# Convolution with channels on the partitions, turned into rows by VectorE

## The chip, the cores and the metric

The kernel runs on one core of a Trainium2 chip. The metric is the device time in microseconds of one execution, as a median of several. TensorE (PE in the profile) does the matmuls and PEld loads their weights; VectorE is DVE, ScalarE is ACT, GpSimd is POOL, and SyncE (SP) issues most transfers. Everything is float32.

## The reference

```python
# x: 8 x 3584 x 192; 8 heads of 24 channels, 7 taps
w = softmax(weight, axis=-1)                    # per head
x = out[b, s] = sum_k w[head, k] * x_pad[b, s + k]      # causal, per channel
# mixture of 8 experts, F = 1024
logits = x @ w_gate
local_gate = sigmoid(x @ w_local)
for b in range(B):
    prev_e = -1
    for s in range(S):
        fresh_e = argmax(logits[b, s])
        e = fresh_e if s == 0 or local_gate[b, s] < 0.5 else prev_e
        prev_e = e
        p = softmax(logits[b, s])
        h = np.maximum(x[b, s] @ w1[e], 0.0)
        out[b, s] = p[e] * (h @ w2[e])
```

A token takes the expert of its own logits or that of the token before it. So the choice is a scan along the sequence, and the tokens must be sorted by expert before the two matmuls with the expert's weights.

## The kernel before

The 28672 tokens are cut into 16 groups of 1792 (`PT`, 128 partitions x 14 tokens). Groups 0 and 1 are convolved by PE at the start (`wide`). Groups 2 to 15 go through these steps:

- `load_x` brings a group's x in one transfer on SP's queue: each partition has 14 tokens and the 6 before them, 192 channels each.
- `conv` makes the convolution with tokens on the partitions. For each of the 8 heads ACT writes the first tap (`first`, L413), and DVE adds the other six (L423, 128 x 336 elements, in place in `y_sb`).
- `logits` turns the rows by DVE transposes of 32 x 32 blocks (`z`, L606), so that channels lie on the partitions. 48 matmuls (L620) with 64 x 32 tiles follow: six slices of channels, four column groups, two halves of the rows. ACT copies the two results to `ls`, DVE turns them back (`lq`, L628), and sixteen small copies put them in order in `lt` (by DVE, L644, or by ACT, L642, where `aside` holds).
- `route` finds expert and factor of each token on DVE, and the slot at which its row is to lie. `put` scatters the 14 rows of `y_sb` a partition to the table `slots` in HBM (L828, POOL's queue). `tables` makes from the counts which block is of which expert.

The sorted rows are worked off in blocks. 28 blocks have one tile of 128 rows and 43 have two (`hidden` L1047, `output` L1068). The 23 large blocks after them have four tiles, and a few smaller ones end the run. Before a block its weights (1.5 MB) and its rows are loaded on SP's queue. `hidden` and `output` split the 128 rows of the contraction into two halves of 64 (`halves`), which run side by side.

A large block computes the hidden layer in `seven`: two by two parts of it, by sums and differences of parts of x and of the weights, in 11 products (`times`, L1211) instead of 12. The three PSUM pairs `xb`, `wbk` and `yb` collect them. ACT copies three intermediate results out (L1217, L1223 and L1225, the last from `xb` to `h12`). DVE then adds `wbk` to `h11` (L1230), `xb` to `h22` (L1233) and `yb` to `h12` (L1242), and ACT applies the ReLU. `output_late` (L1259) follows; its first part writes the PSUM pool that `yb` came from. The pieces `h11` to `h22` are parts of the old tile `hot`, and the sums lie in pieces of old `xg` and `hT` tiles, which is why the profile has these names.

The order of all this is set while the program is written out. `step(time)` is called at fixed places in each block. It takes operations of `route` or `conv` (generators that yield an estimate in microseconds for each DVE operation) until the time given is used up. A yielded "pe" or "hop" hands over to the other generator until the next place. `SIDE` holds the times of the large blocks' four places; the first lies ahead of the additions in `seven`. `start_conv` and `start_route` say when a group may begin:

```python
        free = not any(p[0] <= g - 3 for p in to_put)
        if (st["cgen"] is None and g < NPART and g <= st["route"] + LEAD and free ...
        ...
        if st["rgen"] is None and st["route"] < done:
```

The rows `y_sb` of a group lie in one of four (later three) buffers `ys`, and `z` in the one buffer `yt`.

Of the kernel before, what the change touches and what calls it, by code (L numbers as in the profile page):

```python
# [8 lines left out]
F32 = mybir.dt.float32  # L9
I32 = mybir.dt.int32  # L10
Act = mybir.ActivationFunctionType
# [6 lines left out]
P = 128  # L18
# [3 lines left out]
GS = D // H  # L22
# [73 lines left out]
TQ = (NT + 3) // 4  # L96
WA = F * KD // 2
# [14 lines left out]
def kernel(  # L112
# [4 lines left out]
    weight: bass.AP,  # L117
    wh: bass.AP,
# [49 lines left out]
    c = cst.tile([P, H, KC], F32, name="c")  # L168
    nm = cst.tile([P, H], F32, name="nm")
    rz = cst.tile([P, H], F32, name="rz")  # L170
    with tc.tile_pool(name="scr", bufs=1) as scr:
        w = scr.tile([1, H, KC], F32, name="w")
        nc.scalar.dma_start(out=w, in_=weight.rearrange("(o h) k -> o h k", o=1))

        nc.sync.dma_start(out=hank, in_=wh)
        x_in = {0: load_b(0)}
        wg = cst.tile([P, 3 + DQ, Q], F32, name="wg")
# [15 lines left out]
        wide_w = scr.tile([P, 2 * H + H * KC], F32, name="wide_w")  # L193
# [9 lines left out]
        wc = ws[:, H:].rearrange("o (h k) -> o h k", k=KC)  # L203
        nc.vector.tensor_tensor(w, w, bcast(wm, KC), op=Alu.add)
        nc.scalar.activation(w, w, Act.Exp)
# [5 lines left out]
        nc.vector.tensor_tensor(wc, w, bcast(ws[:, :H], KC), op=Alu.mult)  # L211
        cps = hps_p.tile([P, 512], F32, name="hps")
        nc.tensor.matmul(cps[:, :H + H * KC], lhsT=ones, rhs=wide_w[:, H:], start=True, stop=True)
# [3 lines left out]
    wgb, wgq = wg[:, :3, :], wg[:, 3:, :]  # L217
# [180 lines left out]
    def row_tile(g):  # L398
        at = g % 4 if g < NARROW else (g + 1) % 3
        return ys[at].tile([P, NB, DG], F32, name="y_sb")  # L400

    def conv(g, x_sb):
        y_sb = row_tile(g)[:, :NT, :]
        got[g] = y_sb

        def cols(h):
            return y_sb[:, :, Y0 + h * GS:Y0 + (h + 1) * GS]

        def chans(h, k):
            return x_sb[:, k:k + NT, h * GS:(h + 1) * GS]  # L410

        def first(h):
            nc.scalar.activation(cols(h), chans(h, 0), Act.Copy, scale=c[:, h, 0:1])  # L413

        first(0)
        yield 0
        for h in range(H):
            if h + 1 < H:
                first(h + 1)
            if h == H // 2 and 2 < g < NPART - 1:  # L420
                x_in[g + 1] = load_x(g + 1)
            for k in range(1, KC):
                nc.vector.scalar_tensor_tensor(cols(h), chans(h, k), c[:, h, k:k + 1],  # L423
                                               cols(h), Alu.mult, Alu.add)
                yield 0.6
# [175 lines left out]
    def logits(g, y_sb):  # L601

        z = z_tile()[:, :NT * D].rearrange("p (t d) -> p t d", d=D)
        for t in range(0, NT, TQ):
            u = min(t + TQ, NT)
            nc.vector.transpose(z[:, t:u, :], y_sb[:, t:u, Y0:Y0 + D])  # L606
            yield 0.2 * (u - t)
        yield "pe"


        if late_p:
            both = st["bank"].tile([P, 2, 512], F32, name="ps")
            lps = [both[:, half, :TQ * Q] for half in range(2)]
        else:
            lps = [hps_p.tile([P, TQ * Q], F32, name="hps") for half in range(2)]
        begin = [min(TQ * j, NT - TQ) for j in range(4)]
        for b in range(DQ):
            for j in range(4):
                for half, rows in halves():
# [978 lines left out]
```

## Time and profile before

| | |
|---|---|
| median of 3 runs | 1312.2 us (1310.24 to 1314.26) |
| profiled execution, its own time | 1310.09 us |
| its span | 1308.3 us |
| PE busy | 1274.2 us, 97% |
| DVE busy | 956.2 us, 73% |
| ACT busy | 618.7 us, 47% |
| POOL busy | 551.8 us, 42% |
| mean granted PE clock | 0.996 |

The span runs from the first to the last instruction of the profiled execution. Busy time counts overlapping instructions of an engine once. A row of costs gives line, engine, operation, what is written and read, the shape and the count, then busy microseconds in all, nanoseconds of one, and the idle time just before with what ended it. A matmul of float32 appears as two records.

### The profile page before, as it was taken

What the parts mean: (1) busy time and instruction counts of PE and PEld (TensorE: products, weight loads), DVE (VectorE), ACT (ScalarE), POOL (GpSimd) and SP (SyncE); (2) the same over time, 40 slices, a digit from 0 to 9 for tenths busy, and PEclk for the clock granted to TensorE, in tenths of its full rate; (3) what the DMA queues carried; (4) which work ended last, traced back from release to release, by engine and by line L of the source; (5) the groups of instructions that cost most, each with busy time, mean ns of one, the idle gap of its engine ahead of it and who ended that gap; (6) DMA issues with size and microseconds to landing.
All of it is one profiled execution on the core that took longest, in us unless ns stands there. A gap on an engine that the chain in (4) does not pass through costs nothing. (4 is left out here: it accounts for less than half of the span.)

```text
span 1308.3 us, 40023 instructions
## 1 busy us (share of the span) xinstructions
PE 1274.2 (97%) x15750; PEld 1215.0 (93%) x15750; DVE 956.2 (73%) x2602; ACT 618.7 (47%) x1384; POOL 551.8 (42%) x619
## 2 busy tenths in 40 slices
PE   9899999999999999999999999999999999999997
PEld 7799999999999999899999899999999899999996
DVE  6888898889888888788988898889857844431111
ACT  5345555445555645456464454454343434432332
POOL 4444443534344444444445633644462664421211
PEclk9999999999999999999999999999999999999999
DMA  5789998857767767667696655554555637536894
GB/s 198 279 338 382 375 345 345 295 201 270 259 217 260 264 211 266 221 223 261 206 280 178 171 165 152 152 147 149 127 170 119 192 110 183 157 92 195 269 314 164
DMA packets 130244, 291.18 MB, mean 223 GB/s; under 512 B 87936, under 2 KB 104759, under 8 KB 114306
## 3 DMA queue, kind: packets, MB, share of 16 engines
q1 hardware_dynamic: 107728, 243.35, 56.5%
q0 software_dynamic: 22320, 45.22, 10.3%
q8 instruction: 126, 2.06, 0.7%
q14 instruction: 68, 0.56, 0.1%
q10 hardware_dynamic: 2, 0.00, 0.0%
HBM read 242.92 MB, written 46.07 MB: 221 GB/s over the span
## 5 line engine op out<-in xcount | busy, mean ns | idle before, releaser
L423 DVE SCALAR_TENSOR_TENSOR y_sb<-x_sb,c,y_sb 128x336 f32<-128x336 f32 x672 | 383.1, 579 | 33.9 <-ACT y_sb L413 11.0
L1068 PE MATMUL yps<-wb,hT 64*128 64x192 f32 x3648 | 317.2, 325 | 5.9 <-ACT hT L1056 4.7
L828 POOL DMA_INDIRECT slots<-y_sb,posi x228 | 227.2, 996 | 210.4 <-PE yps L1068 148.4
L1047 PE MATMUL hps<-xT,wb 64*128 64x256 f32 (+1 forms) x3408 | 314.1, 336 | 1.7 <-issue 0.8
L1259 PE MATMUL ps<-wb,hot 64*128 64x192 f32 x3680 | 308.0, 323 | 0.1
L1068 PEld LDWEIGHTS yps<-wb,hT 64*128 64x128 f32 x3648 | 296.5, 187 | 10.4 <-ACT hT L1056 7.1
L1047 PEld LDWEIGHTS hps<-xT,wb 64*128 64x128 f32 x3408 | 279.4, 187 | 25.4 <-issue 4.3
L1259 PEld LDWEIGHTS ps<-wb,hot 64*128 64x128 f32 x3680 | 301.4, 187 | 1.5 <-issue 0.9
L1096 POOL DMA_INDIRECT out_dram<-o_sb,head x115 | 120.7, 1050 | 293.8 <-DVE o_sb L1274 268.1
L1056 ACT ACTIVATE hT<-hps 128x512 f32<-128x512 f32 (+1 forms) x284 | 130.7, 510 | 161.9 <-PE hps L1047 116.4
L1096 POOL DMA_INDIRECT out_dram<-o_sb,xg x114 | 117.2, 1028 | 209.5 <-DVE o_sb L1082 113.8
L1269 ACT ACTIVATE o_sb<-ps,head 128x192 f32<-128x192 f32 x115 | 42.9, 417 | 231.3 <-PE ps L1259 196.7
L1274 DVE SCALAR_TENSOR_TENSOR o_sb<-ps,head,o_sb 128x192 f32<-128x192 f32 x115 | 43.2, 412 | 104.6 <-ACT o_sb L1269 100.3
L1135 DVE STREAM_TRANSPOSE xT<-y_sb 128x768 f32<-128x768 f32 (+1 forms) x65 | 54.8, 870 | 77.3 <-DMA y_sb<-slots 31.4
L1029 ACT COPY xT<-xps 64x256 f32<-64x256 f32 (+4 forms) x284 | 105.1, 370 | 7.6 <-PE yps L1068 1.7
L1078 ACT ACTIVATE o_sb<-yps,xg 128x192 f32<-128x192 f32 x114 | 43.2, 418 | 125.1 <-PE yps L1068 82.9
L1211 PE MATMUL ps<-xT,wb 64*128 64x256 f32 x736 | 88.9, 377 | 0.8 <-DVE xT L1187 0.8
L1211 PEld LDWEIGHTS ps<-xT,wb 64*128 64x128 f32 x736 | 77.2, 187 | 2.6 <-issue 1.6
L1082 DVE SCALAR_TENSOR_TENSOR o_sb<-yps,xg,o_sb 128x192 f32<-128x192 f32 x114 | 43.4, 412 | 32.5 <-ACT o_sb L1078 27.2
L1156 PE MATMUL ps<-xT,wb 64*128 64x128 f32 (+1 forms) x912 | 64.5, 294 | 0.7 <-DVE xT L1135 0.6
L1156 PEld LDWEIGHTS ps<-xT,wb 64*128 64x128 f32 x912 | 62.6, 188 | 1.5 <-DVE xT L1135 1.5
L413 ACT ACTIVATE y_sb<-x_sb,c 128x336 f32<-128x336 f32 x112 | 63.1, 580 | 0.5
(281 smaller groups left out, 1301.2 us busy)
## 6 DMA issues: line engine op xcount, KB each, us to landing
wb<-in_w_dram SPq DMA_DIRECT2D x109, 1536.0 KB
x_sb<-in_x_dram SPq DMA_DIRECT2D x14, 1920.0 KB
y_sb<-slots SPq DMA_DIRECT2D x92, 192.0 KB
xg<-slots SPq DMA_DIRECT2D x43, 195.0 KB
wb<-in_w_dram SPq DMA_DIRECT2D x12, 512.0 KB
slots<-y_sb,posi POOLq DMA_INDIRECT x228
x_sb<-in_xb_dram SPq DMA_DIRECT2D x4, 768.0 KB
y_sb<-slots SPq DMA_DIRECT2D x60, 48.0 KB
```

The costliest lines, as they stand in the source:

```text
L413: nc.scalar.activation(cols(h), chans(h, 0), Act.Copy, scale=c[:, h, 0:1])
L423: nc.vector.scalar_tensor_tensor(cols(h), chans(h, k), c[:, h, k:k + 1], cols(h), Alu.mult, Alu.add)
L828: ins = nc.gpsimd.indirect_dma_start(out=slots[:, :], in_=rows, in_offset=None, out_offset=bass.IndirectOffsetOnAxis(ap=to, axis=0)).ins
L1029: copied = nc.scalar.copy(a, b)
L1047: ins = nc.tensor.matmul(hps[half][:, j, w], lhsT=wb[rows, f0:f0 + P], rhs=xT[rows, d, w], start=(d == 0 and j == 0), stop=(d == KD - 1), ...
L1056: nc.scalar.activation(hT[:, m:m + 2, w], hps[half][:, :, w], Act.Relu)
L1068: ins = nc.tensor.matmul(yps[half][:, k * D:(k + 1) * D], lhsT=hT[rows, m, k * P:(k + 1) * P], rhs=wb[rows, WA + m * D:WA + (m + 1) * D], ...
L1096: sent = nc.gpsimd.indirect_dma_start(out=out, in_=o, in_offset=None, out_offset=bass.IndirectOffsetOnAxis(ap=xg.bitcast(I32)[:, k, 1:2], ...
L1135: nc.vector.transpose(xT.rearrange("p d (j t) -> p j d t", t=Q)[:, js], rows[:, js].rearrange("p j (d t) -> p j d t", t=Q))
L1156: nc.tensor.matmul(hps[:, half, j, :], lhsT=wb[rows, f0:f0 + P], rhs=xT[rows, d, :], start=(d == 0 and j == 0), stop=(d == KD - 1), skip_g ...
L1211: ins = nc.tensor.matmul(to[:, half, j, :], lhsT=b[rows, j * P:(j + 1) * P], rhs=a[rows, :], start=(first and j == 0), stop=True, skip_gro ...
L1259: ins = nc.tensor.matmul(yps[:, half, k * D:(k + 1) * D], lhsT=h[two][rows, side, j, k * P:(k + 1) * P], rhs=wb[rows, f * D:(f + 1) * D], ...
```

## The change

Three things change.

First, the convolution. x comes in a layout made on the host: channel c of 32 on the partition, for each of the four quarters of the rows; then 6 slices of channels, and along each partition 20 x 32 tokens. A tap is then one scalar for each partition and slice (`c`, loaded as `taps` and normalized on the chip, `taps_done`). `conv` has 6 slices instead of 8 heads, with 448 contiguous elements each. Its result is already what the logits matmuls read (`z`; in `ys[2]` for even groups, in `yt` for odd ones). The rows `y_sb` are made from it afterwards, by DVE transposes of the same sizes as before.

Second, the logits. 12 matmuls over all 128 rows replace 48: six slices, two column groups of 64, 224 columns each. There is one copy to `ls`, one transpose, and eight small copies to `lt`.

Third, `seven`: the product a13 b31 is issued in two halves with s3 t3 between them, and `h22` is added ahead of `h11`. The ReLU of `h11` is made in two pieces and that of `h22` last.

With this the row buffers become three (later two), and the rules of starting change.

```diff
     def load_x(g):
-        x_sb = xs.tile([P, NX, D], F32, name="x_sb")
-        src = x[g // PER]
-        win = bass.AP(tensor=src.tensor, offset=src.offset + g % PER * PT * D,
-                      ap=[[NT * D, P], [1, NX * D]])
-        nc.sync.dma_start(out=x_sb.rearrange("p t d -> p (t d)"), in_=win)
-        return x_sb
+        x_sb = xs.tile([P, NX, D], F32, name="x_sb").rearrange("p t d -> p (t d)")
+        nc.sync.dma_start(out=x_sb, in_=x[g])
+        return x_sb.rearrange("p (b s) -> p b s", b=DQ)
...
+        nc.scalar.dma_start(out=c, in_=taps)
...
         nc.vector.tensor_tensor(w, w, bcast(wm, KC), op=Alu.add)
+        nc.vector.tensor_reduce(cz, c, axis=AX.X, op=Alu.max)
+        nc.vector.tensor_tensor(c, c, bcast(cz, KC), op=Alu.subtract)
...
-        nc.vector.tensor_tensor(wc, w, bcast(ws[:, :H], KC), op=Alu.mult)
...
         nc.vector.tensor_copy(rz, cps[:, :H])
-        nc.vector.tensor_copy(c.rearrange("p h k -> p (h k)"), cps[:, H:H + H * KC])
+        nc.scalar.activation(c, c, Act.Exp)
...
+    def taps_done():
+        nc.vector.tensor_reduce(cz, c, axis=AX.X, op=Alu.add)
+        nc.vector.tensor_scalar(cz, cz, 1e-9, None, Alu.add)
+        nc.vector.reciprocal(cz, cz)
+        nc.vector.tensor_tensor(c, c, bcast(cz, KC), op=Alu.mult)
...
     def row_tile(g):
-        at = g % 4 if g < NARROW else (g + 1) % 3
-        return ys[at].tile([P, NB, DG], F32, name="y_sb")
+        return ys[(0, 1, 3)[g % 3] if g < NARROW else g % 2].tile([P, NB, DG], F32, name="y_sb")
+
+    def rows_free(g):
+        return not any(p[0] <= (g - 3 if g < NARROW else g - 2) for p in to_put)
...
-        for h in range(H):
-            if h + 1 < H:
-                first(h + 1)
...
+        for b in range(DQ):
+            if b + 1 < DQ:
+                first(b + 1)
...
             for k in range(1, KC):
-                nc.vector.scalar_tensor_tensor(cols(h), chans(h, k), c[:, h, k:k + 1],
-                                               cols(h), Alu.mult, Alu.add)
-                yield 0.6
+                nc.vector.scalar_tensor_tensor(z[:, b, :], chans(b, k), c[:, b, k:k + 1],
+                                               z[:, b, :], Alu.mult, Alu.add)
+                yield 0.68
...
-    def logits(g, y_sb):
+    def logits(g, z):
...
         for b in range(DQ):
-            for j in range(4):
-                for half, rows in halves():
-                    nc.tensor.matmul(lps[half][Q * j:Q * j + Q, :], lhsT=wgq[rows, b, :],
-                                     rhs=z[rows, begin[j]:begin[j] + TQ, b * Q:(b + 1) * Q],
-                                     start=(b == 0), stop=(b == DQ - 1))
...
+            for j in range(2):
+                nc.tensor.matmul(lps[DR * j:DR * j + DR, :], lhsT=wgq[:, b, :],
+                                 rhs=z[:, b, j * TH * Q:(j + 1) * TH * Q],
+                                 start=(b == 0), stop=(b == DQ - 1))
...
+            nc.vector.transpose(y_sb[:, t:u, Y0:Y0 + D].rearrange("p t (b s) -> p t b s", s=Q),
+                                zt[:, t:u])
+            yield 0.24 * (u - t)
+        st["turned"] = g
...
         put(times(wbk, a12, b21, True))
-        times(wbk, a13, b31)
+        times(wbk, a13, b31, js=[0])
         if st["block"] > FIRST:
             step(SIDE[0], early=1)
-        nc.vector.tensor_tensor(h11, wbk, h11, op=Alu.add)
-        nc.scalar.activation(h11, h11, Act.Relu)
         put(times(xb, s3, t3))
         nc.vector.tensor_tensor(h22, xb, h22, op=Alu.add)
-        nc.scalar.activation(h22, h22, Act.Relu)
+        times(wbk, a13, b31, js=[1])
+        nc.vector.tensor_tensor(h11, wbk, h11, op=Alu.add)
+        for side in range(2):
+            nc.scalar.activation(h11[:, side], h11[:, side], Act.Relu)
         times(yb, s4, b22)
...
         nc.scalar.activation(h21, xb, Act.Relu)
+        nc.scalar.activation(h22, h22, Act.Relu)
...
-        free = not any(p[0] <= g - 3 for p in to_put)
-        if (st["cgen"] is None and g < NPART and g <= st["route"] + LEAD and free
+        if (st["cgen"] is None and g < NPART and g <= st["turned"] + 2
...
-        if st["rgen"] is None and st["route"] < done:
+        if st["rgen"] is None and st["route"] < done and rows_free(st["route"] + 1):
```

The order of the instructions shows where things moved. A row has the line, the operation, what is written and read, the shape of what is written, and a count if it repeats. Line numbers shift a little with the inserted code: L394 becomes L401, L1211 becomes L1213, and L1259 L1263.

On PE, the first large block before (`hot` are the pieces `h11` to `h22`, `xT`, `xg` and `hT` parts and sums of x and weights, `wb` the weights; L1211 are the products, L1259 the output):

```order
L1211 MATMUL ps<-xT,wb 128x256 x12
L1211 MATMUL ps<-xg 128x256 x4
L1211 MATMUL xps<-xT,wb 128x256 x8
L1211 MATMUL ps<-xg 128x256 x4
L1211 MATMUL ps<-hT,wb 128x256 x8
L1211 MATMUL ps<-xT,xg 128x256 x4
L1211 MATMUL ps<-xT,wb 128x256 x4
L1259 MATMUL ps<-wb,hot 128x192 x64
```

And the same block after:

```order
L1213 MATMUL ps<-xT,wb 128x256 x12
L1213 MATMUL ps<-xg 128x256 x4
L1213 MATMUL xps<-xT,wb 128x256 x6
L1213 MATMUL ps<-xg 128x256 x4
L1213 MATMUL xps<-xT,wb 128x256 x2
L1213 MATMUL ps<-hT,wb 128x256 x8
L1213 MATMUL ps<-xT,xg 128x256 x4
L1213 MATMUL ps<-xT,wb 128x256 x4
L1263 MATMUL ps<-wb,hot 128x192 x32
```

Two of the eight matmuls into `xps` (`wbk`) now stand behind s3 t3 (the second row with `xg`). In this block the output stands in two halves, because a group's logits now follow the first.

On DVE, the end of the second large block before (L423 convolution, L1274 the output's second half, L1230, L1233 and L1242 the three additions):

```order
L1191 TENSOR_TENSOR hT<-xT 128x256
L423 SCALAR_TENSOR_TENSOR y_sb<-x_sb,c,y_sb 128x14x24 x3
L1274 SCALAR_TENSOR_TENSOR o_sb<-ps,head,o_sb 128x192 x2
L423 SCALAR_TENSOR_TENSOR y_sb<-x_sb,c,y_sb 128x14x24 x4
L1230 TENSOR_TENSOR hot<-xps,hot 128x1024
L1233 TENSOR_TENSOR hot<-ps,hot 128x1024
L1242 TENSOR_TENSOR hot<-ps,hot 128x1024
```

And the third large block's after, which is the nearest alike:

```order
L1193 TENSOR_TENSOR hT<-xT 128x256
L433 SCALAR_TENSOR_TENSOR z<-x_sb,c,z 128x448 x3
L1278 SCALAR_TENSOR_TENSOR o_sb<-ps,head,o_sb 128x192 x2
L433 SCALAR_TENSOR_TENSOR z<-x_sb,c,z 128x448 x3
L1233 TENSOR_TENSOR hot<-ps,hot 128x1024
L1235 TENSOR_TENSOR hot<-xps,hot 128x1024
L1245 TENSOR_TENSOR hot<-ps,hot 128x1024
```

The addition from `xb` (`ps`) now stands ahead of that from `wbk` (`xps`), and three longer convolution steps stand where four were. Over the whole run, convolution or routing stands ahead of the additions in seventeen of the 23 large blocks before and in ten after; the logits of three groups lie among the large blocks before and of two after.

On PE among the one-tile blocks, a group's logits before (L394 turns the next block's rows):

```order
L394 MATMUL xps<-ident,xg 128x64 x2
L394 MATMUL xps<-ident,xg 64x64 x2
L1068 MATMUL yps<-wb,hT 128x192 x16
L620 MATMUL hps<-z,wg 32x128 x48
L1047 MATMUL hps<-xT,wb 128x128 x24
```

And after:

```order
L401 MATMUL xps<-ident,xg 128x64 x2
L401 MATMUL xps<-ident,xg 64x64 x2
L1070 MATMUL yps<-wb,hT 128x192 x16
L618 MATMUL hps<-y_sb,wg 64x224 x12
L1049 MATMUL hps<-xT,wb 128x128 x24
```

They stand between a block's output and the next block's hidden layer as before, with 12 matmuls instead of 48. The first group's come one block earlier, the last group's after 136 tiles of rows instead of 164.

More of the change, by code (lines that the diff above doesn't have):

```diff
@@ L117 @@
     weight: bass.AP,
+    taps: bass.AP,
     wh: bass.AP,
@@ L191 @@
         awake(3)
-        wide_w = scr.tile([P, 2 * H + H * KC], F32, name="wide_w")
+        wide_w = scr.tile([P, 2 * H], F32, name="wide_w")
         nc.vector.memset(wide_w, 0.0)
@@ L604, in logits @@
         for t in range(0, NT, TQ):
             u = min(t + TQ, NT)
[L606 to L616, printed above, removed]
@@ L1206, in seven, with times @@
             for pool, name in ((late_p[0], "ps"), (xps_p, "xps"), (late_p[1], "ps"))]
-        def times(to, a, b, first=False):
-            for j in range(2):
+        def times(to, a, b, first=False, js=range(2)):
+            for j in js:
                 for half, rows in halves():
```

88 lines of the change are left out of this document (49 added, 39 removed).

## The prediction

> **What bounds the kernel now.** I read the page first, then the busy time by stage, then who makes TensorE (PE) wait, then the costs by shape, and last the timeline of one large block.
>
> ```profile
> span 1308.3 us, 40023 instructions
> ...
> PE 1274.2 (97%) x15750; PEld 1215.0 (93%) x15750; DVE 956.2 (73%) x2602; ACT 618.7 (47%) x1384; POOL 551.8 (42%) x619
> ...
> PE   9899999999999999999999999999999999999997
> ```
>
> PE is busy in 97% of the span and in nearly every slice, while VectorE (DVE) is at 73%. So a microsecond counts only if PE works it or waits it. The trace lists every matmul twice (48 logits matmuls appear as 96 records), so I count records.
>
> ```profile
> 60.00:220.00 160.00, 154.79 (x2497) 149.08 (x2498) 139.48 (x414) 88.13 (x273) 67.96 (x69) 1.00 0.92 355
> 220.00:690.00 470.00, 468.65 (x5858) 439.64 (x5856) 400.42 (x1185) 252.02 (x627) 202.63 (x198) 1.00 0.72 249
> 695.00:1035.00 340.00, 330.45 (x3746) 315.53 (x3744) 282.95 (x674) 152.82 (x234) 164.54 (x177) 1.00 0.55 151
> 1035.00:1157.00 122.00, 121.65 (x1308) 119.42 (x1306) 57.83 (x107) 51.05 (x67) 58.01 (x64) 1.00 0.53 147
> ```
>
> The rows are a stretch, its length, then the busy time of PE, weight load, DVE, ACT and POOL. Blocks of one tile run up to about 220, of two tiles up to 690, large blocks from 695. The two-tile stage leaves PE 1.35 us idle. The large blocks leave it 9.55 us idle while convolution and routing still run on DVE (to about 1035), and 0.35 us afterwards. The later stretch gives the undisturbed pace: 122.00 us for 1308 records, 93.3 ns each. The earlier one has 3746 records, 288 of them logits (4.8 us, quoted below). The other 3458 at 93.3 ns are 322.5 us, and with the logits 327.3 us. The stretch takes 340, so **12.7 us** are lost to disturbance, idle time and refilling after it together.
>
> **The logits matmuls.** Costs by shape, one row for each operation and tile:
>
> ```profile
> L1047 PE MATMUL hps<-xT,wb 64*128 64x256 f32 x2064 | 231.0, 376 | 0.5 <-issue 0.3
> ...
> L620 PE MATMUL hps<-z,wg 64*32 64x128 f32 x1056 | 20.2, 273 | 1.9 <-issue 1.8
> ...
> L244 PE MATMUL hps<-x_sb,wb 118*112 118x192 f32 x64 | 12.2, 331 | 0.0
> ...
> L620 PE MATMUL ps<-z,wg 64*32 64x128 f32 x288 | 4.8, 272 | 0.0
> ```
>
> Before: 20.2 + 4.8 us busy and 1.9 idle are 26.9 us for 14 groups, 1.92 each. Eight 64x32 tiles run at once over 128 columns. After: 12 matmuls of 128 rows by 64 columns over 224 columns each, and only two such tiles fit side by side. No row shows that form. The nearest is the early stage's logits, which use 128-row column tiles (four of 32) already:
>
> ```profile
> 15.00 0.96 PE L275 MATMUL yps<-z,wg 128*32 128x448 f32 x8
> ...
> 15.78 0.94 PE L280 MATMUL yps<-z,wg 128*32 128x224 f32 x16
> 15.78 0.51 PEld L280 LDWEIGHTS yps<-z,wg 128*32 128x32 f32 x12 [0.25 <-issue]
> ```
>
> Four matmuls of 448 columns (8 records) hold PE from 15.00 to 15.78: 0.78 us, so they ran together, at 1.74 ns a column. L1047 says the same: a pair of halves, 4 records of 231.0/2064 = 112 ns, for 256 columns is 1.75. So each of the six channel slices costs 224 x 1.74 = 0.39 us, a group 2.34, and 14 groups 32.8 us. The upper end is L244, full-height matmuls: 12.2/64 x 2 = 0.381 us for 192 columns, 1.99 ns a column, 2.67 a group, 37.4 in all. I take the column tiles' row, it is the same form but for the width: **+5.9 us**, upper end +10.5. The 1.9 us of "issue" I count as gone, since a group now issues 24 records in 2.34 us instead of 96 in 1.9; if it stays, +7.8. Fewer instructions are not fewer columns here: PE streams 224 columns a slice where it streamed 128.
>
> [...]
>
> **The other order of sums.** One undisturbed large block, all engines:
>
> ```profile
> 1075.98 2.79 PE L1211 MATMUL ps<-xT,wb 64*128 64x256 f32 x24
> ...
> 1079.43 1.92 PE L1211 MATMUL xps<-xT,wb 64*128 64x256 f32 x16
> ...
> 1079.76 1.02 ACT L1225 COPY hot<-ps 128x1024 f32<-128x1024 f32 x1
> ...
> 1081.16 1.06 PE L1211 MATMUL ps<-xg 64*128 64x256 f32 x8
> 1081.46 1.22 DVE L1230 TENSOR_TENSOR hot<-xps,hot 128x1024 f32<-128x1024 f32 x1 [3.74 <-PE xps L1211]
> 1082.02 1.92 PE L1211 MATMUL ps<-hT,wb 64*128 64x256 f32 x16
> 1082.60 1.21 DVE L1233 TENSOR_TENSOR hot<-ps,hot 128x1024 f32<-128x1024 f32 x1
> ...
> 1083.96 1.14 PE L1211 MATMUL ps<-xT,xg 64*128 64x256 f32 x8
> 1083.98 1.22 DVE L1242 TENSOR_TENSOR hot<-ps,hot 128x1024 f32<-128x1024 f32 x1 [0.17 <-issue]
> ...
> 1084.90 1.06 PE L1211 MATMUL ps<-xT,wb 64*128 64x256 f32 x8
> ...
> 1085.76 10.60 PE L1259 MATMUL ps<-wb,hot 64*128 64x192 f32 x128
> ```
>
> A product takes 0.86 us (1081.16 to 1082.02). Eleven are 9.49 us; the block takes 9.78 (1075.98 to 1085.76). The 0.29 lies at a22 t4: it could start at 1083.75, but starts at 1083.96, because DVE's second addition (L1233, h22) ends at 1083.81 and must leave the bank first. The product after a wait also starts 0.94 later instead of 0.86. After the change DVE adds h22 first, and half of a13 b31 stands after s3 t3. I walk through it with these durations:
> - s3 t3 comes 0.43 earlier, at 1080.73, but needs ACT's copy of the same bank (L1225, to 1080.78). So it starts at about 1080.83 and the refilling costs another 0.1: a new wait of about 0.2.
> - h22 is added from about 1082.07, h11 from 1083.21, so a22 t4 finds its bank free and loses nothing: 0.29 gained.
> - h12 is DVE's third addition and begins at 1084.35, ending at 1085.57. The output's first matmul writes the bank that it reads. That matmul would be ready at 1085.68 and, with the 0.15 from addition to matmul seen at a22 t4, starts at about 1085.8: 0.04 to 0.1 lost.
>
> So the undisturbed block stays where it is: **0**. The ends for 23 blocks are -6.6 (all 0.29 gone) and +4.6 (the new 0.2 on top of the old).
>
> **The disturbed large blocks.** What made PE wait in them, over the run:
>
> ```profile
> PE ps L1211 <- issue: 6.4, 10, 1.3
> ...
> PE ps L1211 <- DVE hot L1233: 1.6, 1, 1.6
> ...
> PE ps L1211 <- DVE xT L1187: 0.8, 2, 0.6
> PE ps L1211 <- ACT hot L1225: 0.7, 1, 0.7
> ```
>
> "issue" hides two kinds: a22 t4 behind DVE's additions, when DVE comes late from convolution or routing, and s2 t2 behind ACT's first copy, when ACT still moves logits (L642). The order of instructions shows DVE side work ahead of the additions in seventeen of the 23 blocks before and in ten after, with two groups' logits there instead of three. That follows from the changed convolution and start rules: groups are routed earlier, in the two-tile stage, where PE hardly waits. By number, 12.7/17 x 10 = 7.5 us stay. DVE's lateness now counts from 1082.07 instead of 1081.46, 0.6 us forgiven, worth 1.2 us in two late blocks. So 6.3 stay: **-6.4 us**. Ends: 0 and -12.7.
>
> **Work beside PE.**
>
> ```profile
> L423 DVE SCALAR_TENSOR_TENSOR y_sb<-x_sb,c,y_sb 128x336 f32<-128x336 f32 x672 | 383.1, 579 | 33.9 <-ACT y_sb L413 11.0 <-ACT xT L1029 4.7 <-issue 0.6
> ...
> L1082 DVE SCALAR_TENSOR_TENSOR o_sb<-yps,xg,o_sb 128x192 f32<-128x192 f32 x114 | 43.4, 412 | 32.5 <-ACT o_sb L1078 27.2 <-PE yps L1068 1.8 <-PE hps L1047 1.7
> ...
> L642 ACT COPY lt<-lq 32x36 f32<-32x36 f32 x108 | 23.6, 219 | 3.0 <-DVE lq L628 1.5
> ```
>
> Convolution on DVE: 48 x 0.579 = 27.8 us a group before. The two DVE rows give (579 - 412)/144 = 1.16 ns an element, so 448 elements take about 0.70 us, and 36 of them 25.2 us. The transposes stay (same sizes, other direction), 16 small copies become 8. ACT's first taps go from eight to six, and its logits copies from sixteen to eight. All of this is hidden under PE, worth 0 in itself, and shows only through the term above. If DVE's cover failed, its o_sb additions would be late, and PE would wait for yps banks. In the stage from 60 to 220 PE idles 160.00 - 154.79 = 5.2 us, about 1 of it at logits; I take 0 for the rest, ends -4.2 and +4.2.
>
> x is loaded with the same bytes by the same single transfer on SP's queue. Rows of a group are turned only when the scatters of the group three before it (from the ninth on, two before it) are issued, but a group's fourteen scatters stand whole ahead of the next group's on POOL's queue, so nothing new waits there.
>
> **The start.** The added taps transfer stands on ACT's queue behind the weights. DVE reads it before the sums that PE's broadcast needs:
>
> ```profile
> 3.00 2.71 PE L189 MATMUL hps<-ones 128*128 128x128 f32 x14
> ...
> 4.47 0.20 DVE L211 TENSOR_TENSOR wide_w<-w,wide_w 1x56 f32<-1x56 f32 x1
> ...
> 38.81 0.26 DVE L474 COPY nf<-hps 16x112 f32<-16x112 f32 x1 [1.36 <-PE yps L592]
> ```
>
> PE is warming up until 5.7 and DVE is done at 4.67 (L211 itself falls away), so a delay of 1 us is covered. ACT's extra exponential lies just ahead of its first copy out: 0.1 us. The four small operations of taps_done fall into the 1.36 us in which DVE waits for PE. Sum **+0.1**; if the taps come a microsecond later than that cover, +1.
>
> **Sum.** +5.9 + 0 - 6.4 + 0 + 0.1 = -0.4 us. The profiled execution took 1310.09 (span 1308.3), 2.1 below the median of 1312.2. Against that median: 1311.8. Under 0.3%, 3.9 us, a measurement of this kernel can hardly tell from no change.
>
> **Rivals.**
> 1. The new order works as a gain: the copy of L1225 and the addition of h12 are early enough, and the block takes 9.49. Then -6.6 more: 1305.2. For it: both misses are only about 0.1 us. Against: they come from durations that hardly vary.
> 2. The new order is a new wait: DVE's three additions now run in a row up to the output's start, so whatever DVE is late goes to PE. With 0.3 us for 23 blocks it is +6.9: 1318.7, slower. It decides when the output starts more than 5.3 us after s3 t3 (4.60 before, 4.97 by my walk). For it: convolution steps are longer, 0.70 instead of 0.58. Against: thirteen blocks have none ahead of the additions.
> 3. Routing done earlier does not help, and all 12.7 us stay: 1318.2.
> 4. Weight loads in the open, 12 a group at 0.11 us (the L280 loads take about that each): 14 x 1.3 = 18.5 us, 1330.3.
>
> **How the numbers follow.** My case 0.45, with its own range 1307 to 1316; rival 1 0.23; rival 2 0.12; rival 3 0.12; rival 4 0.04; the rest, 0.04, is the early stage by its ends. Faster by over 0.3% (below 1308.3): rival 1, and 0.06 of my case: 0.29. Slower (above 1316.1): rivals 2 to 4 less what they share with no change: 0.25. Within: 0.46. The range 1304 to 1319 takes in rivals 1 to 3.
>
> **What the profile after would show.** The logits matmuls: 33 us busy and next to no idle time ahead of them; over 37 is wrong. An undisturbed large block at 9.8 us from its first product to its output, a short wait at s3 t3 behind ACT's h12 copy and none at a22 t4. Disturbance ending by the eleventh large block, and 6 us lost instead of 12.7. DVE's convolution step at 0.70 us and its total lower by some 40 us. I am wrong if the logits cost nothing more, or if output starts later behind h12.

## The result, and the profile after

The changed kernel takes 1324.5 us (median of 5 runs, 1322.1 to 1328.9), the kernel before beside it 1312.2 (1310.1 to 1315.0). The ratio is 1.0094 with a 95% interval of 1.0073 to 1.0115: slower by 0.9%, some 12 us. The forecast was 1311.8, with a range of 1304 to 1319. The profiled execution of the changed kernel took 1325.8, 1.2 above its median, that of the kernel before 2.1 below its own; so the two traces lie 15.6 us apart, and the accounts below are made in these.

The page of the changed kernel, its span and busy times:

```profile
span 1323.9 us, 37629 instructions
...
PE 1290.5 (97%) x14742; PEld 1212.5 (92%) x14742; DVE 901.8 (68%) x2398; ACT 597.2 (45%) x1294; POOL 556.9 (42%) x619
```

VectorE has 54 us less to do and ScalarE 21 less, as was meant. TensorE, which sets the end, has 16 us more. The same four stretches as in the prediction:

```profile
60.00:220.00 160.00, 155.31 (x2247) 148.52 (x2245) 136.36 (x410) 83.23 (x255) 73.86 (x72) 1.00 0.92 354
220.00:690.00 470.00, 466.96 (x5197) 432.81 (x5195) 403.31 (x1127) 240.64 (x557) 207.63 (x202) 1.00 0.70 249
695.00:1035.00 340.00, 333.99 (x3542) 312.46 (x3540) 228.06 (x552) 143.02 (x217) 172.53 (x184) 1.00 0.56 154
1035.00:1157.00 122.00, 122.00 (x1306) 115.96 (x1304) 52.60 (x85) 50.71 (x72) 43.23 (x49) 1.00 0.53 140
```

The stretches are the same times of the run, in which the changed kernel is up to 21 us further back in its work. TensorE's idle time in the large blocks fell from 9.55 to 6.0 us. In the two-tile stage it rose from 1.35 to 3.0. What made it wait, over the run:

```profile
PE hps L1049 <- issue: 3.4, 10, 0.5
PE yps L1070 <- ACT hT L1058: 3.0, 6, 0.6
PE ps L1213 <- POOL xg L1179: 2.2, 1, 2.2
PE hps L214 <- DVE wide_w L212: 2.1, 1, 2.1
...
PE ps L1213 <- ACT hot L1227: 1.4, 1, 1.4
```

Idle time alone does not add up to 15.6, so I set the starts of the same 113 groups of first-layer matmuls (one group for each block, up to the last few) side by side in the two traces. A logits group is measured from its first matmul to the first matmul behind it.

| from | start before | start after | later by | of the growth: logits | the rest |
|---|---|---|---|---|---|
| first block | 46.3 | 50.0 | 3.7 | | +3.7 |
| 29th (two tiles begin) | 219.7 | 225.9 | 6.2 | +0.3 | +2.2 |
| 72nd (large blocks begin) | 695.2 | 712.7 | 17.5 | +7.4 | +3.9 |
| 113th (near the end) | 1294.2 | 1309.8 | 15.6 | +0.3 | -2.2 |

So 8.0 us are the logits, 3.7 the start, 6.1 other losses in the one-tile and two-tile blocks, and 2.2 are won afterwards. Two executions can differ by some of this. The 2.2 us of the one-tile blocks are missing in the traces of the first and the eighth run below, which issue the same work there (in the eighth with the logits matmuls cut): from the fifth block to the 29th the lateness grows by 2.5 us here, by 0.1 and by 0.0 there.

**The logits.** The rows that stand where the 64x32 tiles stood:

```profile
L618 PE MATMUL hps<-y_sb,wg 128*64 128x224 f32 x144 | 14.9, 357 | 0.0
L618 PE MATMUL hps<-z,wg 128*64 128x224 f32 x144 | 14.9, 357 | 0.0
...
L618 PE MATMUL ps<-y_sb,wg 128*64 128x224 f32 x24 | 2.5, 357 | 0.0
L618 PE MATMUL ps<-z,wg 128*64 128x224 f32 x24 | 2.5, 357 | 0.0
```

34.8 us busy, no idle ahead. All fourteen groups take 2.42 us from first to next, 33.9 together. Before, ten took 1.52 and four 2.1 to 3.7, 25.9 together.

**The start.** TensorE of the kernel before, then of the changed one VectorE, the issue of the transfer, and TensorE:

```profile
5.55 0.33 PE L213 MATMUL hps<-wide_w,ones 128*128 128x64 f32 x2
...
6.37 4.45 PE L244 MATMUL hps<-x_sb,wb 118*112 118x192 f32 x26
```

```profile
3.28 0.19 DVE L204 TENSOR_TENSOR w<-w,wide_w 1x56 f32<-1x56 f32 x1
6.59 0.20 DVE L205 TENSOR_REDUCE cz<-c 128x6 f32<-128x42 f32 x1 [3.11 <-DMA c<-in_taps_dram]
...
7.44 0.19 DVE L212 RECIPROCAL wide_w<-wide_w 1x8 f32<-1x8 f32 x1
```

```profile
1.36 0.36 ACTq L174 DMA_DIRECT2D c<-in_taps_dram  x1
```

```profile
7.68 0.39 PE L214 MATMUL hps<-wide_w,ones 128*128 128x8 f32 x2 [2.05 <-DVE wide_w L212]
...
8.75 5.77 PE L251 MATMUL hps<-x_sb,wb 118*112 118x192 f32 x26
```

The taps, 21 KB issued at 1.36, are there only at 6.59. VectorE stands 3.1 us in front of them with the sums behind it, the broadcast matmul comes at 7.68 instead of 5.55, and then the first 26 convolution records take 5.77 us instead of 4.45. The stretches give the reason for the latter (the granted clock is the third number from the end), before and after:

```profile
8.00:12.00 4.00, 4.00 (x30) 3.98 (x29) 2.69 (x7) 2.53 (x7) 0.61 (x1) 1.00 1.00 343
```

```profile
8.00:12.00 4.00, 4.00 (x17) 3.92 (x17) 1.00 (x3) 0.90 (x3) 0.00 (x0) 0.57 0.99 363
```

TensorE lost its clock behind the wait: it was granted 1.00 in the first 8 us and 0.57 of full speed in the next 4.

**The two-tile blocks.** Around one logits group, ScalarE, VectorE and TensorE:

```profile
305.90 0.35 ACT L622 COPY ls<-hps 128x224 f32<-128x224 f32 x1 [1.71 <-PE hps L618]
311.01 0.51 ACT L645 COPY lt<-lq 32x63 f32<-32x63 f32 x2 [4.76 <-DVE lq L632]
311.42 2.01 ACT L1058 ACTIVATE hT<-hps 128x512 f32<-128x512 f32 x4
```

```profile
306.88 1.83 DVE L627 STREAM_TRANSPOSE y_sb<-y_sb 128x768 f32<-128x768 f32 x2
...
309.25 1.44 DVE L627 STREAM_TRANSPOSE y_sb<-y_sb 128x768 f32<-128x768 f32 x2
310.60 0.38 DVE L632 STREAM_TRANSPOSE lq<-ls 128x224 f32<-128x224 f32 x1
```

```profile
312.05 2.22 PE L1070 MATMUL yps<-wb,hT 64*128 64x192 f32 x24 [0.59 <-ACT hT L1058]
```

`ls` is out at 306.25, but VectorE first turns the rows (L627) and comes to `lq` at 310.60. ScalarE's copies into `lt` are in its queue already and wait 4.76 us; the evictions of the hidden layer stand behind them, and the output waits for these. This happened four times, for 0.5 to 0.6 us each. In the kernel before VectorE had turned the rows ahead of the logits, and `lq` was done 2.5 us before ScalarE came to the copies, which waited for nothing. VectorE and ScalarE around its logits group of 322.88:

```profile
327.56 0.44 DVE L628 STREAM_TRANSPOSE lq<-ls 128x256 f32<-128x256 f32 x1
```

```profile
330.53 1.79 ACT L642 COPY lt<-lq 32x36 f32<-32x36 f32 x8
```

**An undisturbed large block**, all engines:

```profile
1069.93 2.79 PE L1213 MATMUL ps<-xT,wb 64*128 64x256 f32 x24
...
1073.72 1.02 ACT L1227 COPY hot<-ps 128x1024 f32<-128x1024 f32 x1
1074.78 0.73 PEld L1213 LDWEIGHTS ps<-xg 64*128 64x128 f32 x8 [0.31 <-ACT hot L1227]
1074.79 1.13 PE L1213 MATMUL ps<-xg 64*128 64x256 f32 x8
...
1078.31 1.22 DVE L1245 TENSOR_TENSOR hot<-ps,hot 128x1024 f32<-128x1024 f32 x1
...
1079.67 1.57 PE L1263 MATMUL ps<-wb,hot 64*128 64x192 f32 x16
```

From first product to output it takes 9.74 us (9.78 before). s3 t3 waits behind ACT's `h12` copy, as walked through: it starts 4.86 into the block (1074.79), 4.85 was forecast. The output starts 0.14 after DVE's `h12`.

### The profile page after: what moved, and what is told of

Same layout as the page of the kernel before. It is cut to its first block, busy times and chain, and to the rows that moved or that the text cites. A ratio compares the mean times of both kernels' runs of the same rounds, so it can differ in the third digit from the quotient of the medians.

```text
span 1323.9 us, 37629 instructions
## 1 busy us (share of the span) xinstructions
PE 1290.5 (97%) x14742; PEld 1212.5 (92%) x14742; DVE 901.8 (68%) x2398; ACT 597.2 (45%) x1294; POOL 556.9 (42%) x619
## 4 chain that ended last, share of the span: by engine, by line
PE 87%; DVE 6%; DMA 3%; issue 2%; ACT 1%; POOL 0%; another core or an unknown queue 0%; SPq 0%; POOLq 0%; DVEq 0%; ACTq 0%
PE ps L1263 21%; PE hps L1049 21%; PE yps L1070 20%; PE ps L1213 13%; PE ps L1158 4%; PE xps L1213 3%; PE hps L618 2%; DVE y_sb L433 2%; DMA wb<-in_w_dram 1%; DVE z L433 1%; PE xps L401 1%; PE hps L251 1%; DMA y_sb<-slots 1%; DVE y_sb L627 0%; ACT hT L1058 0%
## 5 line engine op out<-in xcount | busy, mean ns | idle before, releaser
L1049 PE MATMUL hps<-xT,wb 64*128 64x256 f32 (+1 forms) x3408 | 317.7, 336 | 3.8 <-issue 3.4
L1263 PE MATMUL ps<-wb,hot 64*128 64x192 f32 x3680 | 309.8, 324 | 0.6 <-ACT hot L1237 0.3
L830 POOL DMA_INDIRECT slots<-y_sb,posi x228 | 232.0, 1018 | 180.2 <-PE yps L1070 111.3
L1263 PEld LDWEIGHTS ps<-wb,hot 64*128 64x128 f32 x3680 | 299.6, 187 | 7.5 <-ACT hot L1237 4.0
L433 DVE SCALAR_TENSOR_TENSOR y_sb<-x_sb,c,y_sb 128x448 f32<-128x448 f32 x252 | 170.7, 687 | 33.3 <-ACT y_sb L423 16.6
L433 DVE SCALAR_TENSOR_TENSOR z<-x_sb,c,z 128x448 f32<-128x448 f32 x252 | 173.9, 699 | 28.3 <-ACT z L423 12.2
L1213 PE MATMUL ps<-xT,wb 64*128 64x256 f32 x736 | 88.4, 376 | 0.8 <-DVE xT L1189 0.8
L1233 DVE TENSOR_TENSOR hot<-ps,hot 128x1024 f32<-128x1024 f32 x23 | 28.2, 1224 | 76.3 <-PE ps L1213 71.4
L1213 PEld LDWEIGHTS ps<-xT,wb 64*128 64x128 f32 x736 | 75.7, 187 | 3.9 <-issue 1.5
L1237 ACT ACTIVATE hot<-hot 128x512 f32<-128x512 f32 x46 | 26.4, 622 | 85.8 <-DVE hot L1235 77.8
```

The source lines that it names most:

```text
L433: nc.vector.scalar_tensor_tensor(z[:, b, :], chans(b, k), c[:, b, k:k + 1], z[:, b, :], Alu.mult, Alu.add)
L830: ins = nc.gpsimd.indirect_dma_start(out=slots[:, :], in_=rows, in_offset=None, out_offset=bass.IndirectOffsetOnAxis(ap=to, axis=0)).ins
L1049: ins = nc.tensor.matmul(hps[half][:, j, w], lhsT=wb[rows, f0:f0 + P], rhs=xT[rows, d, w], start=(d == 0 and j == 0), stop=(d == KD - 1), ...
L1213: ins = nc.tensor.matmul(to[:, half, j, :], lhsT=b[rows, j * P:(j + 1) * P], rhs=a[rows, :], start=(first and j == 0), stop=True, skip_gro ...
L1263: ins = nc.tensor.matmul(yps[:, half, k * D:(k + 1) * D], lhsT=h[two][rows, side, j, k * P:(k + 1) * P], rhs=wb[rows, f * D:(f + 1) * D], ...
```

## The experiments

All were timed in rounds against the kernel before, whose median lay between 1309.0 and 1313.4 us beside them, so ratios are compared (0.001 is 1.3 us). Lateness "start to start" is read from the traces as in the table above.

**1. The taps' arithmetic behind the routing of group 0.** Changed kernel, with

```diff
-        nc.vector.tensor_reduce(cz, c, axis=AX.X, op=Alu.max)
-        nc.vector.tensor_tensor(c, c, bcast(cz, KC), op=Alu.subtract)
...
-        nc.scalar.activation(c, c, Act.Exp)
...
     rest(route0)
+    taps_exp()            # the three operations
     some(wide1, WIDE - 20)
```

> Changed kernel (1324.5 us) with the maximum, subtraction and exponential of the taps moved from the start to behind the routing of group 0; the transfer stays where it is. Theory: the first block begins 3.7 us later than before (50.0 against 46.3) because VectorE waits 3.1 us for this transfer, TensorE then idles 2 us and runs the next matmuls at half their rate. So the first block begins at 46.3 to 46.8 again and the kernel takes 1320.8. Rival: the start is later for another reason (the matmul of the sums, the order of the weights' transfers behind one more transfer), then the first block begins at 49 or later and the time stays above 1323. Second rival: what is gained at the start is lost in the routing of group 1 that follows, and the first block moves back by less than 1.5 us.

Measured: 1330.7 us, ratio 1.0126 (1.0103 to 1.0148), no faster than the changed kernel. The start was mended (broadcast at 6.1, clock 1.00 up to 15 us), and the loss came back as another one. ScalarE:

```profile
33.80 0.24 ACT L220 ACTIVATE c<-c 128x42 f32<-128x42 f32 x1 [7.01 <-DVE c L219]
33.94 0.95 ACT L278 COPY z<-hps 128x448 f32<-128x448 f32 x2
```

and TensorE:

```profile
34.51 0.95 PE L284 MATMUL yps<-z,wg 128*32 128x448 f32 x1 [6.30 <-issue]
```

The exponential was put into ScalarE's queue where VectorE had 7 us of routing ahead of its subtraction. Two copies of group 1's transposes stood behind it, and TensorE waited 6.3 us for them ("issue" names nobody; the copy of 33.94 does). My own edit made the very kind of wait that it was to remove.

**2. The same, in a gap.** The two VectorE operations go behind the last copy of group 0's logits, the exponential two products later:

```diff
     some(wide0, 1)
+    nc.vector.tensor_reduce(cz, c, axis=AX.X, op=Alu.max)
+    nc.vector.tensor_tensor(c, c, bcast(cz, KC), op=Alu.subtract)
     some(wide1, 2)
+    nc.scalar.activation(c, c, Act.Exp)
     rest(wide0)
```

> Changed kernel with the taps' maximum and subtraction on VectorE just behind the last copy of group 0's logits (where it stood idle 0.9 us) and the exponential on ScalarE behind two more products of group 1. Theory: the later start is the wait for the taps' transfer alone; the matmul with the sums comes at 5.9 as before the change, the first block begins at 46.3 to 47.2 instead of 50.0, and the kernel takes 1320.5 to 1322. Rival: the first block hangs on something else that also moved (the other places of the changed routing and scatters, 48 to 50 again), time within 1 us of 1324.5.

Measured: ratio 1.0067 (1.0048 to 1.0086), about 3.5 us better than the changed kernel by the medians, though the two intervals overlap. TensorE at the start:

```profile
6.21 0.41 PE L212 MATMUL hps<-wide_w,ones 128*128 128x8 f32 x2
...
7.01 4.39 PE L248 MATMUL hps<-x_sb,wb 118*112 118x192 f32 x26
```

No wait, full pace again, and the first block begins at 45.2, 1.1 earlier than in the kernel before; the lead is gone by the fourth block (TensorE waits 2.9 us for VectorE's `o_sb` there). That the later start is the taps' wait is shown by the traces.

**3. 48 matmuls again.** Changed kernel with the old form of the logits on the new layout:

```diff
-            for j in range(2):
-                nc.tensor.matmul(lps[DR * j:DR * j + DR, :], lhsT=wgq[:, b, :],
-                                 rhs=z[:, b, j * TH * Q:(j + 1) * TH * Q], ...)
+            for j in range(4):
+                for half, rows in halves():
+                    nc.tensor.matmul(lps[half][Q * j:Q * j + Q, :], lhsT=wgq[rows, b, :],
+                                     rhs=z[rows, b, begin[j] * Q:(begin[j] + TQ) * Q], ...)
```

> Changed kernel with the logits as before the change: 48 matmuls of 64x32 tiles over 128 columns, 16 small copies instead of 8. Everything else as changed. Theory: TensorE streams 128 columns a slice instead of 224; a group takes 1.45 to 1.55 us instead of 2.42, 14 groups 12 us less; the time is 1312 to 1316, less 12 if the issue gaps of 1.9 us before the change do not return, less 8 if they and the lost microseconds around them do. Rival: the logits' matmuls lie beside other waits (TensorE waits for VectorE anyway), then TensorE's waits grow by what its matmuls shrink and the time stays above 1321.

Measured: 1.0091 (1.0074 to 1.0109), no gain; the rival's time. Yet the groups took 26.5 us start to start instead of 33.9. What took most of the 7.4 us is in the waits:

```profile
PE yps L1077 <- ACT hT L1065: 8.2, 4, 2.7
PE hps L1056 <- issue: 3.3, 7, 0.9
PE ps L1165 <- DVE xT L1144: 3.2, 2, 1.8
PE hps L623 <- issue: 2.4, 6, 0.9
```

The form brings back sixteen copies on ScalarE and the gaps of "issue" ahead of the matmuls. The wait behind `hT` grew from 3.0 to 8.2 and that behind `xT` at the end from 1.7 to 3.2. The undo was not of one thing.

**4. The copies one place later.** Changed kernel with

```diff
-        if aside and late_p:
+        if aside:
             yield "hop"
```

> Changed kernel, where in the two-tile blocks too the copies into lt on ScalarE are given out one place later than the transpose lq that they read. Theory: in the changed kernel VectorE turns the rows ahead of lq, ScalarE's first copy waits 3 to 5 us for it with the evictions of the hidden layer behind it, and TensorE waits in the output (yps L1070 behind hT L1058: 2.2 us busy-free in 4 places, some 0.7 each start to start). The four waits go, 1321.5 to 1322.5. Rival: the copies then meet the next place's work and ScalarE waits there; the row on hT stays at 2 us or more and the time within 1 us of 1324.5.

Measured: 1.0065 (1.0049 to 1.0082), some 3.8 us better by the medians, with intervals that overlap. The trace is clearer. The waits behind `hT` in the two-tile blocks are gone; from the 29th to the 72nd block the lateness grows by 8.7 us instead of 11.3.

**5. All three, with the misplaced exponential of the first run.**

> Changed kernel with all three: taps' arithmetic later, 48 matmuls for the logits, copies into lt one place later. Theory: the three costs are apart in place and add up: -3.7, -8 to -12, -2.5, so 1306 to 1310, faster than the kernel before (1312.2) by the large blocks' gain alone, 3 to 5 us. Rival: what the large blocks gained comes from having fewer matmuls and small copies there; then it goes with them and the time is 1312 to 1314.

Measured: 1.0066 (1.0047 to 1.0084). Most of the miss is the start: TensorE's 6.3 us of waiting stand in its trace too, and the twelfth run below, which differs only there, gives 1.0018. That is still behind the kernel before, where 1306 to 1310 us would have been ahead of it.

**6. The order of sums alone, in the kernel before** (as in the diff of `seven`).

> Kernel before (1312.2 us) with the new order of sums in the large blocks, nothing else changed. Theory: an undisturbed block gains and loses the same (a new short wait at s3 t3, the old one at a22 t4 gone), and the later point from which VectorE's lateness counts forgives 0.6 us in the one or two late blocks: 1310 to 1312, TensorE's waits behind L1225 and L1233 change places. Rival 1: the order is a gain of 0.29 a block, 1305 to 1306. Rival 2: three additions in a row ahead of the output make a new wait, 1316 or more, seen as the output waiting for VectorE's or ScalarE's h12.

Measured: 1.0000 (0.9986 to 1.0014). Neither rival.

**7. The old order of sums in the changed kernel.**

> Changed kernel (1324.5 us) with the old order of sums in the large blocks. Theory: the large blocks' gain of the changed kernel (3.5 to 5 us over 23 blocks) comes from fewer blocks with convolution or routing ahead of the additions, not from the order of sums: 1324 to 1326. Rival: the gain is the order's: 1328 or more, as the large blocks lose what they gained.

Measured: 1.0096 (1.0079 to 1.0113) against 1.0094. Both ways round the order of sums is worth nothing that can be measured. The quiet block is 9.74 us with the new order and 9.79 with the old, 1 us over 23 blocks. What the large blocks gained is thus not the order's. The forgiveness of 0.6 us in late blocks that I had counted on is not seen either.

**8. Twice the weight loads for the same columns.** Each logits matmul cut in two:

```diff
+            for half in range(2):
                 for j in range(2):
-                    nc.tensor.matmul(lps[DR * j:DR * j + DR, :], ...  # 224 columns
+                    c0 = half * TH * Q // 2
+                    nc.tensor.matmul(lps[DR * j:DR * j + DR, c0:c0 + TH * Q // 2], ...  # 112
```

> Changed kernel with each of the twelve logits matmuls cut into two of 112 columns: the same columns, twice the weight loads. Theory (TensorE's time goes by columns streamed, loads lie underneath): a group stays at 2.4 to 2.5 us from first to last, the time at 1324 to 1327. Rival (each load of 128 rows stands in the open behind the matmul ahead, about 0.11 us): twelve more loads make a group 3.7 us, 14 groups 18 us more: 1342.

Measured: 1.0082 (1.0067 to 1.0097), not slower than the changed kernel. The logits' rows:

```profile
L620 PE MATMUL hps<-z,wg 128*64 128x112 f32 x288 | 15.5, 261 | 0.3 <-issue 0.3
L620 PE MATMUL hps<-y_sb,wg 128*64 128x112 f32 x288 | 15.1, 261 | 0.0
```

A group takes 2.45 us start to start against 2.42, with twelve loads more (one of the fourteen took 3.1). The fourth rival, that the loads stand in the open (an assumption that no trace had shown), is out. With tiles of all 128 rows, side by side in two column groups, the twelve loads more cost 0.03 us a group here, against the 1.3 us that it counted for twelve.

**9. The logits twice.** The twelve matmuls done two times over.

> Changed kernel with the twelve logits matmuls of each group done twice over (the second pass starts the sums anew; the result is the same). Theory: TensorE has no slack here, so the columns cost one for one, 2.35 us a group: 14 groups 33 us, 1355 to 1359. Rival: a part lies under waits that TensorE has anyway, 15 us or less more: under 1340.

Measured: 1.0292 (1.0270 to 1.0315), 26 us more than the changed kernel. In the trace the groups grew from 33.9 to 65.7 us. By the medians 26 of 31.8 arrive at the end, four fifths; between the two traces 21.4 do, two thirds. So it is neither one for one nor the rival's half. Of the 10 us that are missing between the traces, 4.5 went in the two-tile blocks and 3.8 in the large ones. There two groups grew by 4.5 us and the lateness only by 0.7.

**10. Start and copies mended together.**

> Changed kernel with the taps' arithmetic in that gap and the copies into lt one place later. Theory: the start (-3) and the waits behind ScalarE in the two-tile blocks (-2, measured when mended alone) are apart and add up: 1319 to 1320. What is left to the kernel before is the logits' own columns, 14 groups at 0.9 us. Rival: mended together they are worth no more than one of them, 1322.

Measured: 1.0064 (1.0046 to 1.0082), no more than the second run. In the traces the copies' place is worth 2.7 us from the 29th to the 72nd block here too. But two of the later groups then come to their logits one block earlier, and the first large block loses 2.1 us instead of 0.6. In all four kernels with this edit it lost 2.1, in the others that start from the changed one 0.5 to 1.3, and 1.7 with `lq` first (below). By times alone the mend on top of the other stays unsettled; the intervals are as wide as it is.

**11. Why the copies waited: `lq` first.** The second run's kernel, with VectorE's turning of the rows behind the copies instead of ahead of `lq`:

```diff
         nc.scalar.copy(ls, lps)
-        (turn the rows: L624 to L630)
+        yield "hop"
         lq = ...
         ... copies into lt
+        (turn the rows)
         return y_sb, lt
```

> Changed kernel with the taps' arithmetic in the gap (1.0067 of the kernel before), and the logits' transpose lq and the copies into lt given out ahead of the transposes that turn the rows, one place after the matmuls. Theory: ScalarE's copies waited because VectorE turned the rows first; with lq first they find it done, the waits behind hT in the two-tile blocks go (2.2 us in the profile, 2.7 start to start) and nothing is handed back in the first large block, where moving the copies alone cost 1.4: ratio 1.004 to 1.005. Rival: the turning, now later, delays the end of routing and the next convolution by as much, and the ratio stays at 1.0065 or goes above.

Measured: 1.0079 (1.0057 to 1.0101): the rival's time, the theory's mechanism. No wait behind `hT` is left in the two-tile blocks, and they lose 8.9 us instead of 11.1. But from the fifth block to the 29th, with one tile, the lateness grows by 5.0 us instead of 0.6. TensorE's waits there:

```profile
PE yps L1068 <- ACT hT L1056: 1.7, 4, 0.6
PE hps L1047 <- issue: 1.6, 6, 0.4
PE yps L1068 <- DVE o_sb L1082: 0.7, 1, 0.7
```

That VectorE's turning ahead of `lq` held up ScalarE is shown. Its other place seems to cost as much elsewhere; of the 4.4 us more in the one-tile blocks up to 2.5 can be the difference between two executions that was seen above.

**12. All three, with the taps in the gap.**

> Changed kernel with the taps' arithmetic in that gap, the copies one place later, and 48 matmuls of 64x32 tiles. Theory: 48 matmuls alone gained nothing because they bring back 16 copies on ScalarE, which stood between TensorE and the evictions of the hidden layer (5.6 us against 2.2); once the copies stand one place later the columns saved do count, 0.9 us a group: 8 to 11 us below the kernel with the two other mends, 1309 to 1312, level with the kernel before or just under it. Rival: TensorE's shorter logits are filled by other waits, and the time is 1317 or more.

Measured: 1312.7 us, 1.0018 (1.0001 to 1.0034), the best of these and level with the kernel before or just behind it. Against the tenth run the 48 matmuls now gain 6 us, clear of both intervals: the theory's way, but short of its 8 to 11. The wait behind `hT` is small over the whole run, and none of it lies in the two-tile blocks:

```profile
PE hps L620 <- issue: 1.7, 6, 0.4
...
PE yps L1074 <- ACT hT L1062: 1.3, 2, 0.9
```

In its trace the two-tile blocks still fall 4.9 us further behind the kernel before (2.0 of them at the logits, of which one group more lies there), and the large blocks and the end win nearly 7 back.

**13. 48 matmuls with `lq` first.**

> The same order with 48 matmuls of 64x32 tiles and 16 copies, and the taps' arithmetic in the gap. With copies one place later this stood at 1.0018. Theory: the 16 copies find lq done, the logits cost 21 to 26 us in 14 groups and the gain in the large blocks stays: 0.998 to 1.000, level with the kernel before or just faster. Rival: as with 12 matmuls, the later turning takes it back, 1.002 or more.

Measured: 1.0041 (1.0027 to 1.0054). The rival: as in the eleventh run, this order does not pay. No version beat the kernel before.

## Why the prediction was wrong

| term | forecast | in the two traces |
|---|---|---|
| logits | +5.9 | +8.0 |
| large blocks, first product to output, quiet and disturbed | 0 and -6.4 | -5.2 (237.2 to 232.0 for 23) |
| work beside PE, two-tile blocks | 0 | +3.9 |
| work beside PE, one-tile blocks | 0 (ends -4.2 and +4.2) | +2.2 |
| start | +0.1 | +3.7 |
| what lies outside, from the large blocks' outputs on | none | +3.0 |
| sum | -0.4 | +15.6 |

- **The start** is the first step that failed: "so a delay of 1 us is covered". The cover was right, the size of the delay was not. VectorE began to wait at 3.5 and the transfer landed at 6.6; the sums stood behind the wait. The only small transfer on ScalarE's queue in the kernel before is the 0.2 KB of weights, issued at 0.82 and read by VectorE at 2.11, 1.3 us later; the taps took 5.2. One such row was no ground for an upper end of 1 us. That TensorE ran at 0.57 of its clock behind this wait was missed too: of the 3.7 us, 2.4 are the later beginning of the convolution (8.75 instead of 6.37) and 1.3 its slower pace.
- **Work beside PE** is the second: "all of this is hidden under PE, worth 0 in itself". I counted that sixteen copies become eight and not what they stand behind. The prediction named VectorE's `o_sb` additions as the place where a failure would show; it showed at ScalarE's evictions. The change puts four transposes (three of 0.95 us and one of 0.54) ahead of `lq` on VectorE and takes the "hop" away that had stood ahead of `lq`. The fourth, eleventh and thirteenth runs show it: the wait behind `hT` goes with either of two edits. It accounts for 2.6 or 2.7 of the 3.9 us; the rest stays without a cause.
- **The logits** were right in kind and mis-sized by 2 us: 2.42 us a group against 2.34 forecast, and the old groups took 25.9 and not 26.9. The gaps that I "count as gone" did go (0.0 ahead of the logits). The waits by "issue" in the hidden layers grew from 0.8 to 3.4 us, but all ten lie inside the hidden layers of one-tile blocks, and none directly behind a logits group.
- **The undisturbed block**: right, with its new wait, its lost old one and its 9.74 us. Rivals 1 and 2 fell with runs 6 and 7.
- **The disturbed blocks**: about right. Over their fastest block's pace the 23 lost 12.5 us before and 8.4 after (6 were forecast), the last of them the eleventh, as forecast; in the other runs of the changed kernel it was 4.5 (the eleventh) to 10.0 us (the eighth), so the forecast size lies within what differs between these runs. Rival 3, that all of it stays, is out. In the ninth large block TensorE waits 2.2 us for POOL's L1179. That does not refute "so nothing new waits there", on POOL's queue: POOL is idle for 0.84 us just ahead of L1179 (at 889.01) and is released by TensorE, and so is ScalarE's first copy of the block (L1219, at 888.95), which comes 3.92 us into the block instead of the 1.15 of the undisturbed one. Why both are released so late is open, and it was not so in every run (1.1 to 1.2 us lost in that block in runs 2, 9, 10, 11 and 12).
- **Convolution on DVE**: 0.687 and 0.699 us a step against 0.70 forecast; VectorE's total fell by 54 us, not 40.
- Open: 1.3 of the 3.0 us outside are `xT` transposes late at the end (a wait of 1.7 us in two places); the rest, and the 2.2 us in the one-tile blocks, were not traced to a cause. The latter did not come in every run.

The two signs on which the prediction's list ends, logits that cost nothing more and an output later behind `h12`, both stayed away. What failed lay where no sign had been set.

The general fault: what had no price in the trace (a small transfer at the start, a copy whose source comes later) I set to nothing, where the ends should have stood far apart. The change relieved VectorE and ScalarE, which had room (68% and 45% busy in the trace after), and gave columns to TensorE, which had little (97%).

## What to carry to other kernels

Fewer instructions on the engine that bounds were no gain where they streamed more columns: twelve matmuls of 224 columns, two side by side, took 2.42 us a group, 0.9 more than 48 of 128 columns, eight side by side (1.52 in ten groups of fourteen). For each small operation that moves, ask what stands behind it in its own engine's queue and what it waits for; 0.5 us of copies that waited 4.76 us for their source held back the evictions behind them, and an edit that undoes a cost can plant the same trap again (the first run). Undo one thing at a time: 48 matmuls looked worthless until the copies that came with them had another place.

## What the runs showed of the hardware

- 21 KB on 128 partitions, issued on ScalarE's queue at 1.36 us beside the first loads, landed 5.2 to 5.8 us later in the traces of the changed kernel and of the third, fourth, seventh and eighth runs, in which VectorE waits for it (it goes on at 6.59 to 7.15).
- TensorE lost its clock after waits of 1.65 to 2.5 us at the start (0.51 to 0.62 from 8 to 12 us) and kept it after one of 1.59. Whether the length of the wait or its place in time decides is not shown. In the changed kernel the lost clock costs 1.3 us on top of the wait (5.77 against 4.45 for the first 26 records). TensorE in the seventh run, whose wait did not cost the clock (1.00 from 8 to 12 us):

```profile
8.00 0.39 PE L214 MATMUL hps<-wide_w,ones 128*128 128x8 f32 x2 [1.59 <-DVE wide_w L212]
...
8.77 4.39 PE L251 MATMUL hps<-x_sb,wb 118*112 118x192 f32 x26
```

- Two matmuls of 128 rows by 64 columns side by side kept a pace of 1.8 ns a column, whether cut at 224 (2.42 us for 6 x 224) or at 112 columns (2.45).
